# Another order for the softmax differences, the counting steps and a product on POOL

## The chip, the cores and the metric

The kernel runs on one core of a Trainium2 chip. The metric is the device time of one execution in microseconds (us); all times below are in us unless marked ns. TensorE is called PE (its weight loads PEld), VectorE DVE, ScalarE ACT, GpSimd POOL and SyncE SP. L12 is line 12 of the kernel.

## The reference, cut to what matters

Two mixers read the same x (2048 tokens, 512 columns, 32 heads of 16) and a gate per token blends them.

```
g = sigmoid((x * gate_w).sum(-1))
# A: linear attention, phi = softmax(p) beside softmax(-p), over 16 columns a head
phi_q, phi_k = ...
kv = einsum("bhsf,bhsd->bhfd", phi_k, v);  z = einsum("bhsf->bhf", phi_k)
den = einsum("bhqf,bhf->bhq", phi_q, z) + 1e-6
a = (einsum("bhqf,bhfd->bhqd", phi_q, kv) / den) @ wo
# B: 32 heads choose one expert of 16 x 16 each, by the best score of either half
act = gelu(einsum("nd,nhkd->nhk", x, u[best]));  b = sum of act * v[best] over heads
out = g * a + (1 - g) * b
```

## The kernel before, in words

The tokens are 16 tiles of 128. A first part (to about 130) folds the weights and gathers kv and z over all tiles. The second part, which the change touches, is a loop over tiles in which the stages of different tiles overlap. The order on every engine is the order of the program text, written out by hand; each engine works through its own queue and waits at semaphores.

For one tile t the work is:

- PE multiplies x by the folded query weights (`front_q`, tile `pq`, 12 matmuls of 512 columns), by the expert scores (`front_s`, two halves `s`, 12 each) and by the expert inputs and the gate (`front_p`, `pp`, 12 of 258 columns).
- `soft_in` (L670) makes the dual softmax's inputs with `softmax_diffs` (L111) on DVE: maximum (L115), minimum (L117), high difference p - max (L119), low difference min - p (L121). Between these four steps it calls a function `step`, by which other work is dealt in. `soft_exp` (L685) is two exponentials on ACT, one for each difference. `soft_w` (L691) is two products with z on POOL (`w`), one for each half. `soft_sum` (L695) sums the exponentials, `soft_y` (L705) sums w, both on DVE. `soft_p` (L700) makes 1e-6 times the product of both sums, as a third column beside two. `soft_b` (L707) turns these into the weight of each half: a product (L713), a sum over three columns (L715), a reciprocal (L717) and a product with the gate (L719) on DVE, then two products over the exponentials on POOL (L726).
- `planes`, `join`, `mid_num`: ACT splits the weighted exponentials into 16-bit planes (L758), SP transposes them by DMA, ACT joins them (L768), PE multiplies by kv (L777, `oT`). `num_hi` (L784, ACT) and `num_lo` (L790, DVE) split the result into a high and a low part for the output product.
- `best` (L734, L735) on DVE finds where each head's score is its maximum, once for each half. `turn_eq` (L741) transposes this by DMA into `et`, and `mid_mask` (L798, `mk`) on PE turns it into bit masks. `count` (L802 to L835) is a chain of 17 small DVE steps that counts, for each of the 256 experts, how many heads chose it. `step(t, n)` runs n steps of this chain and `drain(t)` the rest.
- `gelu_pre` (ACT), `gelu_in` (POOL, L653), `gelu_act` (ACT, L657 to L659) and `gelu_out` (POOL, L663) make the gelu of all 256 experts. `coef` (L839) on POOL multiplies it by the count. `c_planes` (L844), `c_join` (L851, L855) and `back_cl` (L876, DVE) turn, join and split this coefficient.
- `back` is 18 matmuls of the output (L888, L895, tile `po`), `store` (L912) copies it out.

A stage `turned(a)` (L971) does the softmax of tile a, the scores of tile n = a + 1, the counting, gelu and coefficient of tile b = a - 1 and the output of earlier tiles (z = a - 2). Of the 18 matmuls of an output some are put off: each stage up to 7 does 15 of them, each from 8 on 18. Five counting steps of tile a run within `soft_b(a)`; the twelve others run in the next stage within `soft_in`, dealt out by `dealt` (L960): after the maximum the gate reciprocal (L649), five steps and `back_cl` (L876), after the minimum five, after the high difference two.

On POOL the order of a stage is L653 of tile a, L691 twice, L663 and L839 of tile b, then L726 twice. `z_final` (L920) sums z over partitions on PE and copies it into `zb`, which `soft_w` reads.

Stages 0 and 1 and the tail (tile 15 with what is left of 13 and 14) are written out beside the loop and call `soft_in` without dealt work (in stage 15 counting steps follow it).

Of the kernel before, what the change touches and what calls it, by code (L numbers as in the profile page):

```python
# [15 lines left out]
AF = mybir.ActivationFunctionType  # L16
ALU = mybir.AluOpType
AX = mybir.AxisListType
# [17 lines left out]
def mix_kernel(ctx, tc, xT, wqT, wkT, wv, wphi, wo, wq, kk, ug, ev, cst, out):  # L36
    nc = tc.nc
    pe, dve, act, pool, sp = nc.tensor, nc.vector, nc.scalar, nc.gpsimd, nc.sync
# [4 lines left out]
    def mm_bank(name):  # L43
        return psum.tile([P, 512], F32, tag="mm", bufs=4, name=name)

    def tr_bank(name):
        return psum.tile([P, 512], F32, tag="tr", bufs=3, name=name)
# [27 lines left out]
    def x_of(t):  # L75
        first = max(f for f in SEC if f <= t)
        return tuple(xt[i, first][:, t - first] for i in range(2))
# [30 lines left out]
    def proj(o, t, wh, wl, c0, c1, ks=range(NK)):  # L108
        mm3(o, [(*xs(t, k), wh[:, k, c0:c1], wl[:, k, c0:c1]) for k in ks], ks[0] == 0, ks[-1] == NK - 1)
# [58 lines left out]
    class Sums:  # L168
        h = ((gh, gl), x_of(NT - 1))
# [152 lines left out]
    st8 = {t: {} for t in range(NT)}  # L322

    def front_s(t, half):
        e = st8[t]
        e[half] = mm_bank(f"s{half}_{t}")
        proj(e[half], t, sh, sl, 512 * half, 512 * half + 512)
# [141 lines left out]
    for t in range(5, NT - 1, 2):  # L469
# [14 lines left out]
        a = pks[t] = mm_bank(f"pk{t}")  # L484
        prod(a, tile_of(t, 0), b11, True)
        b = mm_bank(f"pu{t}")
# [23 lines left out]
        c = mm_bank(f"pv{t}")  # L510
# [65 lines left out]
    t = NT - 1  # L576
# [33 lines left out]
    zb = w2.tile([P, 1024], F32, name="zb", bufs=1)  # L610
    chains = {}

    def step(t, n=1):
        for _ in range(n):
            if t in chains and next(chains[t], None) is None:
                del chains[t]

    def drain(t):
        while t in chains:
            step(t)  # L620
# [22 lines left out]
    def gelu_pre(t):  # L643
        gelu_gate(t)
        gelu_rest(t)

    def gate(t):
        gs = st8[t]["g"]
        yield dve.reciprocal(gs[:, 2:3], gs[:, 1:2])  # L649
# [11 lines left out]
    def gelu_out(t):  # L661
        px, x2 = st8[t]["G"], st8[t]["x2"]
        pool.tensor_tensor(px, x2, px, op=ALU.mult)  # L663
# [16 lines left out]
    pair = lambda a: a.rearrange("p (h s) -> p h s", s=2)  # L680
# [6 lines left out]
    def soft_w(t):  # L687
        e = st8[t]
        e["w"] = w2.tile([P, 1024], F32, tag="w", bufs=1, name=f"w{t}")
        for i in range(2):  # L690
            pool.tensor_tensor(hs(e["w"], i), hs(e["ph"], i), hs(zb, i), op=ALU.mult)  # L691
# [2 lines left out]
        e = st8[t]  # L694
        dve.tensor_reduce(pair(e["st"][:, 64:128])[:, :, 1 - i], hs(e["ph"], i), axis=AX.X, op=ALU.add)  # L695

    def soft_p(t):
        st = st8[t]["st"]
        sm = pair(st[:, 64:128])
        dve.scalar_tensor_tensor(st[:, 128:224].rearrange("p (h c) -> p h c", c=3)[:, :, 2], sm[:, :, 0], 1e-6,  # L700
                                 sm[:, :, 1], op0=ALU.mult, op1=ALU.mult)

    def soft_y(t, i):
        e = st8[t]
        dve.tensor_reduce(pair(e["st"][:, 224:288])[:, :, i], hs(e["w"], i), axis=AX.X, op=ALU.add)  # L705

    def soft_b(t, step=step):  # L707
        e = st8[t]
        d, st = e["ph"], e["st"]
        sm, y, n_ = pair(st[:, 64:128]), pair(st[:, 224:288]), st[:, 288:320]  # L710
        q3 = st[:, 128:224].rearrange("p (h c) -> p h c", c=3)
        step(t)
        dve.tensor_tensor(q3[:, :, 0:2], y, sm, op=ALU.mult)  # L713
        step(t)
        dve.tensor_reduce(n_, q3, axis=AX.X, op=ALU.add)  # L715
        step(t)
        dve.reciprocal(n_, n_)  # L717
        step(t)
        dve.scalar_tensor_tensor(y, sm, e["g"][:, 2:3], n_.unsqueeze(2).to_broadcast([P, H, 2]),  # L719
                                 op0=ALU.mult, op1=ALU.mult)  # L720
        r = st[:, 224:288]
        step(t)
        for i, s_ in enumerate(halves):
            eng = dve if t == NT - 1 else pool
            gs_ = slice(32 * i, 32 * i + 32)
            eng.tensor_tensor(g64(d)[:, gs_], g64(d)[:, gs_], r[:, gs_].unsqueeze(2).to_broadcast([P, 32, F]), op=ALU.mult)  # L726
# [110 lines left out]
    def coef(t):  # L837
        e = st8[t]
        (pool if t < NT - 1 else dve).tensor_tensor(e["C"], e["C"], e["G"], op=ALU.mult)  # L839
# [34 lines left out]
    def back_cl(t, eng=dve):  # L874
        ch, cl, o = st8[t]["c"]
        eng.tensor_tensor(cl, o[:, :2 * P], ch, op=ALU.subtract)  # L876
# [43 lines left out]
    def z_final(zh, zl):  # L920
        for i, s_ in enumerate(halves):
            o = tr_bank("z")
            pe.matmul(o, neg, zh[i], start=True, stop=False)
            pe.matmul(o, neg, zl[i], start=False, stop=True)
            act.copy(zb[:, s_], o)

    def wo_load():
        both = late.tile([P, 2, D], F32, tag="d", name="rawo2")
# [29 lines left out]
    z_final(zh, zl)  # L958
    gelu_rest(0)
    def dealt(a, b, z):  # L960
        def first():
            for _ in gate(a):
                step(b)
            step(b, 4)
            if z >= 0:
                back_cl(z, dve)

        moves = iter((first, lambda: step(b, 5), lambda: step(b, 2), lambda: None))
        return lambda: next(moves)()

    def turned(a):  # L971
        n, b, z = a + 1, a - 1, a - 2
        owed = min(18, 3 * max(0, a - DEFER))
        left = min(18, 3 * max(0, a - DEFER + 1))
        if a == 2:
            mid_num(z)
            num_hi(z)
            gelu_pre(a)
        planes(b, 0)
        c_join(z)  # L980
        planes(b, 1)
        front_q(a)
        if owed:
            back(z - 1, owed)
            store(z - 1)
        gelu_in(a)
        if a == 2:
            num_lo(z)
        soft_in(a, dealt(a, b, z))
        drain(b)  # L990
        gelu_act(a)
        front_s(n, 0)
        if a < 5:
            if a == 2:
                front_s(n, 1)
            else:
                mid_num(z)
                num_hi(z)
            if a == 3:
                front_s(n, 1)  # L1000
            mid_mask(a)
            if a > 3:
                front_s(n, 1)
            soft_exp(a)
        else:
            soft_exp(a)
            mid_num(z)
            num_hi(z)
            mid_mask(a)
            front_s(n, 1)  # L1010
        soft_w(a)
        soft_sum(a, 0)
        soft_sum(a, 1)
        if a > 2:
            num_lo(z)
        front_p(n, False)
        if left < 18:
            back(z, 18 - left)
        best(n, 0)
        soft_y(a, 0)  # L1020
        soft_y(a, 1)
        soft_p(a)
        join(b)
        gelu_out(b)
        coef(b)
        c_planes(b)
        soft_b(a)
        best(n, 1)
        turn_eq(n)
        gelu_pre(n)  # L1030

    for a in range(NT - 1):
        n, b, z = a + 1, a - 1, a - 2
        if a > 1:
            turned(a)
            continue
        B, Z = b >= 0, z >= 0
        if a == 1:
            front_q(a)
            v15 = vproj(NT - 1)  # L1040
            act.copy(woh[3], rawo[3])
            planes(b, 0)
            v15()
            planes(b, 1)
        gelu_in(a)
        for _ in gate(a):
            pass
        if B:
            soft_in(a)
            dve.tensor_tensor(wol[3], rawo[3], woh[3], op=ALU.subtract)  # L1050
            step(b, 3)
            soft_exp(a)
            front_s(n, 0)
            mid_mask(a)
            kvacc(NT - 1)
            kv_final()
            cl_.close()
            w4 = ctx.enter_context(tc_pool("w4", "right"))
        else:
            gelu_act(a)  # L1060
        if not B:
            pass
        front_s(n, 1)
        front_p(n, False)
        soft_w(a)
        if B:
            best(n, 0)
        soft_sum(a, 0)
        soft_sum(a, 1)
        if B:  # L1070
            drain(b)
            soft_y(a, 0)
            soft_y(a, 1)
            soft_p(a)
            join(b)
            gelu_out(b)
            coef(b)
            c_planes(b)
            gelu_act(a)
            soft_b(a)  # L1080
            best(n, 1)
            turn_eq(n)
        else:
            pool.tensor_tensor(wol[2], rawo[2], woh[2], op=ALU.subtract)
            step(a, 5)
            best(n, 0)
            best(n, 1)
            turn_eq(n)
            soft_y(a, 0)
            soft_y(a, 1)  # L1090
            soft_p(a)
            soft_b(a, lambda t: None)
            gelu_pre(n)
    a, b, z = NT - 1, NT - 2, NT - 3
# [11 lines left out]
    def both(*ts):  # L1106
        for t in ts:
            step(t)
# [32 lines left out]
    soft_y(a, 0)  # L1141
    step(b, 2)
    soft_y(a, 1)
    soft_p(a)
    soft_b(a, lambda t: both(b, a))
    drain(b)
    coef(b)
# [85 lines left out]
```

## Time and profile before

| | us |
|---|---|
| median of 3 runs | 374.69 |
| lowest and highest | 374.16, 375.67 |
| the profiled execution | 375.6 |
| its span, first to last instruction | 373.8 |
| mean granted PE clock | 0.995 |
| busy: PE, DVE, ACT, POOL | 363.2, 338.2, 257.7, 205.2 |

A row of an order of time reads: start, duration, engine, line, operation, tile written, tile read, shapes, count; in brackets the engine's idle time before it and what released it. Where two instructions of a kind follow each other they stand in one row with x2 and their common duration. A matmul's end is modelled, so the pace of PE is read from the starts. A row on DVE can begin a little before the one ahead of it ends, so what an instruction costs its engine is also read from starts. Records of POOL are rough.

### The profile page before, as it was taken

Reading aid. Unit: us, or ns where it says so; the run is one execution under the profiler, and the core shown is the slowest. Engines: PE = TensorE matmul, PEld = TensorE weight load, DVE = VectorE, ACT = ScalarE, POOL = GpSimd, SP = SyncE. Lnnn points to the kernel's source line nnn. Section 1 sums busy time; section 2 is a strip of 40 time slices with the busy share of each in tenths; the row PEclk is TensorE's granted clock in tenths of the full one; section 3 lists DMA queues with packets and bytes.
Section 4 is the critical chain, followed back from the end, with each engine's and each line's share of the span. In section 5 each row is a group of like instructions: output and inputs, shape, how many; then the busy total and the mean of one; then the engine's idle time right before and its main releaser. Section 6 shows DMA issues by size and latency. Waiting matters only on the chain.

```text
span 373.8 us, 8800 instructions
## 1 busy us (share of the span) xinstructions
PE 363.2 (97%) x3426; PEld 284.0 (76%) x3426; DVE 338.2 (90%) x757; ACT 257.7 (69%) x457; POOL 205.2 (55%) x207
## 2 busy tenths in 40 slices
PE   8999999999989999999999999999999999999696
PEld 4766767777858878887787788878878888888476
DVE  4679999999788889999999999999999999999983
ACT  4585678876654776778687668767767776787843
POOL 1079989988846846444544445437426435454800
PEclk9999999999999999999999999999999999999899
DMA  7867888657882214044263442361551532522612
GB/s 269 317 243 264 278 257 228 198 145 283 289 164 86 70 20 82 20 84 83 60 114 70 72 112 50 80 128 26 102 116 27 114 82 61 113 63 68 98 44 84
DMA packets 74729, 47.32 MB, mean 127 GB/s; under 512 B 66240, under 2 KB 67136, under 8 KB 72384
## 3 DMA queue, kind: packets, MB, share of 16 engines
q1 hardware_dynamic: 73824, 45.89, 46.9%
q10 hardware_dynamic: 864, 0.87, 0.8%
q8 instruction: 27, 0.44, 0.5%
q14 instruction: 14, 0.11, 0.1%
HBM read 26.43 MB, written 4.19 MB: 82 GB/s over the span
## 4 chain that ended last, share of the span: by engine, by line
PE 68%; DVE 18%; DMA 4%; issue 4%; POOL 3%; ACT 2%; ACTq 0%; POOLq 0%
PE po L888 9%; PE pk L459 5%; PE po L895 4%; PE s L56 4%; PE s L57 4%; PE s L58 4%; PE ws L292 4%; PE pu L459 4%; PE pq L57 2%; PE pq L56 2%; PE pq L58 2%; DMA et<-eq 2%; PE pe L459 2%; PE kvacc L283 2%; PE pv L459 2%
## 5 line engine op out<-in xcount | busy, mean ns | idle before, releaser
L691 POOL TENSOR_TENSOR w<-d,zb 128x512 f32<-128x512 f32 x32 | 41.1, 1304 | 71.2 <-ACT d L685 71.2
L56 PE MATMUL s<-sh,xh 128*128 128x512 f32 x128 | 51.3, 400 | 0.0
L57 PE MATMUL s<-sl,xh 128*128 128x512 f32 x128 | 50.0, 390 | 0.0
L726 POOL TENSOR_TENSOR d<-d,st 128x512 f32<-128x512 f32 x30 | 31.2, 1063 | 34.0 <-DVE st L719 32.6
L58 PE MATMUL s<-sh,xl 128*128 128x512 f32 x128 | 49.8, 389 | 0.0
L758 ACT COPY pl<-d 128x1024 uint16<-128x1024 uint16 x30 | 31.3, 1044 | 20.7 <-POOL d L726 20.7
L685 ACT ACTIVATE d<-d 128x512 f32<-128x512 f32 x32 | 20.0, 631 | 28.5 <-DVE d L119 20.3
L768 ACT COPY pt<-tp 128x1024 uint16<-128x1024 uint16 x30 | 39.0, 1374 | 0.0
L276 POOL TENSOR_TENSOR d<-d,st 128x1024 f32<-128x1024 f32 x16 | 32.0, 2001 | 10.5 <-DVE st L272 7.4
L58 PEld LDWEIGHTS s<-sh,xl 128*128 128x128 f32 x128 | 24.0, 188 | 5.1
L56 PEld LDWEIGHTS s<-sh,xh 128*128 128x128 f32 x128 | 24.0, 188 | 4.8 <-ACT ctj L851 0.2
L57 PEld LDWEIGHTS s<-sl,xh 128*128 128x128 f32 x128 | 24.1, 188 | 4.5
L56 PE MATMUL pq<-wah,xh 128*128 128x512 f32 x64 | 25.2, 393 | 0.0
L156 DVE TENSOR_TENSOR xl<-xr,xh 128x512 fp32r<-128x512 f32 (+2 forms) x17 | 23.5, 1397 | 1.7 <-ACT xh L152 1.6
L58 PE MATMUL pq<-wah,xl 128*128 128x512 f32 x64 | 25.0, 390 | 0.0
L57 PE MATMUL pq<-wal,xh 128*128 128x512 f32 x64 | 25.0, 390 | 0.0
L735 DVE TENSOR_TENSOR eq<-s,mx 128x512 bf16<-128x512 f32 x32 | 22.1, 691 | 1.1
L695 DVE TENSOR_REDUCE st<-d 128x32 f32<-128x512 f32 x32 | 21.6, 681 | 1.3
L734 DVE TENSOR_REDUCE mx<-s 128x32 f32<-128x512 f32 x32 | 21.8, 680 | 0.0
L271 DVE TENSOR_REDUCE st<-d 128x64 f32<-128x1024 f32 x16 | 19.3, 1209 | 2.2 <-ACT d L267 2.2
L267 ACT ACTIVATE d<-d 128x1024 f32<-128x1024 f32 x16 | 17.0, 1065 | 5.8 <-DVE d L121 5.8
L705 DVE TENSOR_REDUCE st<-w 128x32 f32<-128x512 f32 x32 | 20.5, 676 | 0.6 <-POOL w L691 0.6
(273 smaller groups left out, 1121.8 us busy)
## 6 DMA issues: line engine op xcount, KB each, us to landing
wq<-wq SPq DMA_DIRECT2D x16, 1024.0 KB, 6.0
xr<-xT SPq DMA_DIRECT2D x15, 256.0 KB, 5.2
y<-ot SPq DMA_DIRECT2D x15, 256.0 KB, 2.4
rawk<-wkT SPq DMA_DIRECT2D x1, 1024.0 KB, 6.5
rawq<-wqT SPq DMA_DIRECT2D x1, 1024.0 KB, 6.8
rawu<-ug SPq DMA_DIRECT2D x2, 258.0 KB, 6.1
rawv<-wv ACTq DMA_DIRECT2D x2, 256.0 KB, 4.6
rawv<-wv SPq DMA_DIRECT2D x2, 256.0 KB, 5.8
```

What stands on the lines that cost most here:

```text
L56: pe.matmul(o, ah, bh, start=(first and i == 0), stop=False)
L57: pe.matmul(o, ah, bl, start=False, stop=False)
L58: pe.matmul(o, al, bh, start=False, stop=(last and i == n - 1))
L156: dve.tensor_tensor(l[:, ks], rawx[t][:, ks], h[:, ks], op=ALU.subtract)
L276: pool.tensor_tensor(g64(d), g64(d), b64(st[:, 128:192]), op=ALU.mult)
L459: pe.matmul(o, x_, w_, start=(first and i + j == 0), stop=(i == 1 and j == 2), skip_group_check=True)
L691: pool.tensor_tensor(hs(e["w"], i), hs(e["ph"], i), hs(zb, i), op=ALU.mult)
L726: eng.tensor_tensor(g64(d)[:, gs_], g64(d)[:, gs_], r[:, gs_].unsqueeze(2).to_broadcast([P, 32, F]), op=ALU.mult)
L735: dve.tensor_tensor(e["eq"][:, 512 * half:512 * half + 512].rearrange("p (h f) -> p h f", f=F), p3, mx.unsqueeze(2).to_broadcast([P, H, F] ...
L758: act.copy(pl, e["ph"][:, halves[i]].bitcast(U16).rearrange("p (c j) -> p j c", j=2))
L768: act.copy(p16[:, :, 4 * i:4 * i + 4, :], e["tp"][i].rearrange("p (j g) n -> p j g n", j=2))
L888: pe.matmul(po, a, b, start=(i == 0), stop=False)
```

## The change

It reorders and it leaves one instruction out.

- In the loop, `dealt` hands out the work in another way: nothing after the maximum; the gate reciprocal alone after the minimum; two counting steps after the high difference; after the low difference one counting step, `back_cl` and all the other steps. The high difference thus directly follows maximum, minimum and reciprocal.
- `gelu_out(b)` and `coef(b)` move ahead of `soft_w(a)`. On POOL the order of a stage becomes L653, L663, L839, L691 twice, L726 twice (lines of before).
- The 1e-6 of the denominator is no longer made of the two sums (`soft_p` is gone in all tiles, the sum L715 runs over two columns). Half of it is added to each z by the copy in `z_final`, since the two softmaxes of a head sum to 2.

```
-    def soft_p(t):
-        dve.scalar_tensor_tensor(st[:, 128:224].rearrange("p (h c) -> p h c", c=3)[:, :, 2], sm[:, :, 0], 1e-6,
-                                 sm[:, :, 1], op0=ALU.mult, op1=ALU.mult)
...
-        q3 = st[:, 128:224].rearrange("p (h c) -> p h c", c=3)
+        q2 = pair(st[:, 128:192])
-        dve.tensor_tensor(q3[:, :, 0:2], y, sm, op=ALU.mult)
+        dve.tensor_tensor(q2, y, sm, op=ALU.mult)
-        dve.tensor_reduce(n_, q3, axis=AX.X, op=ALU.add)
+        dve.tensor_reduce(n_, q2, axis=AX.X, op=ALU.add)
...
-            act.copy(zb[:, s_], o)
+            act.activation(zb[:, s_], o, AF.Copy, bias=0.5e-6)
...
     def dealt(a, b, z):
-        def first():
-            for _ in gate(a):
-                step(b)
-            step(b, 4)
-            if z >= 0:
-                back_cl(z, dve)
-        moves = iter((first, lambda: step(b, 5), lambda: step(b, 2), lambda: None))
+        def after_min():
+            for _ in gate(a):
+                pass
+        def after_high():
+            step(b, 2)
+        def after_low():
+            step(b)
+            back_cl(z, dve)
+            drain(b)
+        moves = iter((lambda: None, after_min, after_high, after_low))
         return lambda: next(moves)()
...
         soft_in(a, dealt(a, b, z))
-        drain(b)
...
+        gelu_out(b)
+        coef(b)
         soft_w(a)
...
         soft_y(a, 1)
-        soft_p(a)
         join(b)
-        gelu_out(b)
-        coef(b)
         c_planes(b)
```

More of the change, by code (lines that the diff above doesn't have):

```diff
@@ L695, in soft_sum @@
         dve.tensor_reduce(pair(e["st"][:, 64:128])[:, :, 1 - i], hs(e["ph"], i), axis=AX.X, op=ALU.add)
-    def soft_p(t):
-        st = st8[t]["st"]
-        sm = pair(st[:, 64:128])
-        dve.scalar_tensor_tensor(st[:, 128:224].rearrange("p (h c) -> p h c", c=3)[:, :, 2], sm[:, :, 0], 1e-6,
-                                 sm[:, :, 1], op0=ALU.mult, op1=ALU.mult)
     def soft_y(t, i):
@@ L1073, in mix_kernel @@
             soft_y(a, 1)
-            soft_p(a)
             join(b)
@@ L1090, in mix_kernel @@
             soft_y(a, 1)
-            soft_p(a)
             soft_b(a, lambda t: None)
@@ L1143, in mix_kernel @@
     soft_y(a, 1)
-    soft_p(a)
     soft_b(a, lambda t: both(b, a))
```

## The prediction

> **What bounds the kernel now.** I read, in this order, the busy time of the engines, the table by windows, the order of time on DVE, POOL, PE and ACT, and the chain that ended last.
>
> ```profile
> PE 363.2 (97%) x3426; PEld 284.0 (76%) x3426; DVE 338.2 (90%) x757; ACT 257.7 (69%) x457; POOL 205.2 (55%) x207
> 187.48:202.07 14.59, 14.59 (x107) 12.02 (x106) 14.11 (x39) 10.72 (x21) 6.78 (x8) 1.00 0.44 82
> 347.60:360.00 12.40, 8.97 (x99) 6.72 (x99) 12.33 (x36) 9.21 (x16) 6.44 (x8) 0.86 0.51 86
> ```
>
> The last two lines are windows: length, then busy time of PE, PEld, DVE, ACT and POOL, then the granted clock. In a stage of the main loop PE and DVE are both full. Right after the loop, from 347.60 on, DVE is still full, while PE idles and its clock falls to 0.86. So it has to be asked who leads whom. DVE in stage 4, and the same line a stage later and at the start of the tail:
>
> ```profile
> 186.88 0.68 DVE L115 TENSOR_REDUCE st<-pq 128x32 f32<-128x512 f32 x1
> 187.78 0.89 DVE L820 TENSOR_TENSOR X<-m 128x256 uint32<-128x256 uint32 x1
> 193.54 0.68 DVE L121 TENSOR_TENSOR d<-st,pq 128x512 f32<-128x512 f32 x1
> 194.14 1.46 DVE L695 TENSOR_REDUCE st<-d 128x32 f32<-128x512 f32 x2
> 195.52 0.74 DVE L790 TENSOR_TENSOR xl<-oT,xh 128x256 fp32r<-128x256 f32 x2
> 197.50 1.27 DVE L705 TENSOR_REDUCE st<-w 128x32 f32<-128x512 f32 x2
> 198.69 0.19 DVE L700 SCALAR_TENSOR_TENSOR st<-st 128x32 f32<-128x32 f32 x1
> 198.79 0.21 DVE L807 CAST sa<-mk 128x64 uint16<-128x64 f32 x1
> 201.48 0.68 DVE L115 TENSOR_REDUCE st<-pq 128x32 f32<-128x512 f32 x1
> 347.57 0.67 DVE L115 TENSOR_REDUCE st<-pq 128x32 f32<-128x512 f32 x1
> ```
>
> A DVE stage lasts 201.48 - 186.88 = 14.60, and from stage 4 to the tail (347.57) there are eleven of 14.61: a metronome with no wait in it. PE over the same stretch:
>
> ```profile
> 179.88 0.39 PE L888 MATMUL po<-wbh,xh 128*128 128x512 f32 x1
> 180.11 0.40 PE L888 MATMUL po<-wbl,xh 128*128 128x512 f32 x1
> 181.39 0.73 PE L888 MATMUL po<-t1h,xl 128*128 128x512 f32 x2 [0.89 <-DVE xl L790]
> 182.43 0.39 PE L56 MATMUL pq<-wah,xh 128*128 128x512 f32 x1
> 196.48 0.39 PE L56 MATMUL pq<-wah,xh 128*128 128x512 f32 x1
> 208.90 0.29 PE L57 MATMUL pp<-ul,xh 128*128 128x258 f32 x1
> 209.02 0.29 PE L58 MATMUL pp<-uh,xl 128*128 128x258 f32 x1
> 209.79 0.50 PE L888 MATMUL po<-t1h,xh 128*128 128x512 f32 x1 [0.48 <-ACT xh L784]
> 269.00 0.39 PE L56 MATMUL pq<-wah,xh 128*128 128x512 f32 x1
> 342.63 0.39 PE L56 MATMUL pq<-wah,xh 128*128 128x512 f32 x1
> 345.14 0.39 PE L58 MATMUL pq<-wah,xl 128*128 128x512 f32 x1
> 351.82 0.38 PE L798 MATMUL mk<-wm,et 128*128 128x16 bf16 x8 [3.43 <-DMA et<-eq]
> 353.06 0.63 PE L895 MATMUL po<-eh,ch 128*128 128x512 f32 x1
> 353.49 0.63 PE L895 MATMUL po<-el,ch 128*128 128x512 f32 x1
> ```
>
> An early PE stage, which carries 15 products of the output, takes 196.48 - 182.43 = 14.05. A late one carries 18 and takes (342.63 - 269.00) / 5 = 14.73. So DVE leads up to stage 7 and PE, at its own full pace, after it. A product follows another after 0.23 (179.88 to 180.11), a short one after 0.12 (208.90 to 209.02). PE's idle time before the tail is two stalls: 181.39 - 180.11 - 0.23 = 1.05 (the low part from DVE came late) and 209.79 - 209.02 - 0.12 = 0.65 (the high part from ACT). The scores of tile 15 end at 345.14 + 0.39 = 345.53 on PE, but DVE takes them up at 347.57, 2.0 behind. The tail then waits for DVE twice over: PE stands 3.43 until the transposed maxima of tile 15 arrive, and afterwards it runs products 0.43 apart (353.06 to 353.49) instead of 0.23.
>
> **The change, part by part.** *High differences earlier (L119 behind L117, L121 two counting steps later).* No instruction is added; the same 12 counting steps, the gate reciprocal and the low coefficient part are dealt out in another order, and as many of them as before follow directly on their own source (nine, by the code), so the order by itself costs nothing. What changes is whom they meet:
>
> ```profile
> L820 DVE TENSOR_TENSOR X<-m x15: 424/895/997, 147.1 to 350.7; 128x256 uint32<-128x256 uint32 x15
> 187.65 0.74 POOL L653 TENSOR_TENSOR x<-x,px 128x256 f32<-128x256 f32 x1
> 193.71 2.56 POOL L691 TENSOR_TENSOR w<-d,zb 128x512 f32<-128x512 f32 x2 [5.32 <-ACT d L685]
> 196.22 0.75 POOL L663 TENSOR_TENSOR px<-x,px 128x256 f32<-128x256 f32 x1
> 197.05 0.74 POOL L839 TENSOR_TENSOR cf<-cf,px 128x256 f32<-128x256 f32 x1
> 359.39 0.42 DVE L835 TENSOR_TENSOR cf<-X 128x256 f32<-128x256 uint8 x1
> 359.95 0.74 POOL L839 TENSOR_TENSOR cf<-cf,px 128x256 f32<-128x256 f32 x1 [4.90 <-DVE cf L835]
> ```
>
> L820 takes 0.424 at its fastest and 0.895 at the median (the first row: fastest, median, slowest). At 187.78 it starts while POOL's gelu product L653 runs (187.65 to 188.39) and ends at 188.67, its short time after POOL is through. In the new order two reductions and one difference come ahead (0.60 each, as from 193.54 to 194.14), the gate reciprocal and L813 (0.3 together), so L820 starts some 2.1 after L115, at about 188.97 on this stage's scale. That gains 0.47.
>
> But the gelu output product L663 now follows L653 without a wait, at about 188.34 to 189.09, and the step L813 ahead of L820 comes at 188.75. If it is held as L820 was, whose end was 0.28 after POOL's, it loses 0.2. Bounds: 0 (POOL already through, as when DVE waits for PE) and 0.35. I take 0.2 where DVE leads, nothing where it waits for PE. The Trainium skill, "SBUF — State Buffer", Who interferes with whom, says that a Vector instruction with two SBUF inputs and a GpSimd instruction that reads SBUF exclude each other for the whole instruction. By that L813 would lose the 0.35 and the DVE stage below would be 14.17; the trace agrees on the blocking but shows L820's release 0.14 sooner than POOL's record ends.
>
> *Exponentials earlier.* The pair of sums L695 takes 1.38 to its successor (194.14 to 195.52), the pair L705 only 1.19 (197.50 to 198.69), because the second sum waits for the second exponential. In the new order ACT gets both differences over 3 us before the sums: 0.18 gained.
>
> *soft_p gone, L715 over 64 in place of 96 columns.* L700 starts 0.10 ahead of L807, so dropping it saves 0.10 and not its 0.19, since neighbours overlap; 32 columns fewer save about 0.03, an estimate from the 0.60 that 512 columns take. This holds in all 16 tiles. Adding 0.5e-6 to z happens once, inside a copy that ACT makes anyway: 0, and 0.1 at most.
>
> *Coefficient ahead of the softmax weights.* POOL's L663 and L839 move ahead of L691, and L839 waits for the last counting step L835. Queued behind it on POOL are both halves of L691, and DVE's L705 waits for those. From the end of L835: 0.14 to the start of L839 (359.39 + 0.42 to 359.95), 0.83 to the next instruction (as from 196.22 to 197.05), 2.56 for the pair: w complete at 3.53. DVE wants the second half after the sums (1.20), the low part and the next tile's maximum (195.52 to 197.50, 1.98) and the first y sum (0.60), less 0.08 overlap: 3.70. It fits by 0.2, so 0; in stage 2, where the low part is elsewhere, it misses by about 0.5, once. c_planes, on ACT behind join, and its transpose on SP come no later than before.
>
> A DVE stage thus becomes 14.60 - 0.47 + 0.20 - 0.18 - 0.13 = 14.02. That is below PE's 14.05 and 14.73: **PE becomes the bound** of the whole loop. Over stages 3 to 14 DVE would gain 12 x 0.58 = 7.0, far more than the 2.0 that it lags; the rest is not cashed.
>
> *Where it ends.* PE's two stalls go (low part and high part both come over 1 us sooner): -1.7, bounds 0 and -2.0. DVE takes the scores of tile 15 at 345.53 - 1.7 = 343.8 plus 0.05: 3.7 sooner than 347.57. If the stalls stay, it is 2.0. Then the tail, with these rows:
>
> ```profile
> DMA to landing us min/median/max: 2.7/2.7/4.4
> 364.41 0.75 DVE L790 TENSOR_TENSOR xl<-oT,xh 128x256 fp32r<-128x256 f32 x2 [0.84 <-ACT xh L784]
> 360.72 0.62 ACT L844 COPY plc<-cf 128x512 uint16<-128x512 uint16 x1 [1.22 <-POOL cf L839]
> 362.04 1.07 ACT L751 COPY pt<-pt 128x512 f32<-128x512 f32 x2 [0.70 <-PE pt L749]
> ```
>
> The maxima of tile 15 do not need its scores, so they leave DVE near 342.9 (343.85 - 14.73 for L115 of stage 14, and 13.82 for a stage of DVE's in which L813 is not held), and their transpose, by the first row 2.7 to 4.4 on its way, lands at 345.6 to 347.3. PE wants it at 351.82 - 3.43 - 1.7 = 346.7 and so stands 0.6 at most instead of 3.43. A stall of 0.89 (at 181.39) was followed by products at the full pace, so I also count the slow ones as cured: PE alone could be over 5 us sooner. DVE and ACT can't: L835 moves by 3.7 + 0.1 = 3.8, with it coefficient, L844 and L751 on ACT. There the 0.70 that ACT now waits for PE goes too, since PE is ahead, and the 0.84 of DVE behind it. So the last output tile comes 3.8 + 0.7 = **4.5 us** sooner. The profiled execution took 375.6 (span 373.8), 0.9 over the median 374.69 of runs from 374.16 to 375.67; its span would be 369.3 and it would take 371.1, and the median 370.2.
>
> **Rivals.** *PE keeps its stalls* (the low and high parts stay late, or a bank comes free late). For it: PE has no other slack to give. Against it: both releasers move by more than the stalls. Then DVE gains its 2.0 lag alone: 2.0 + 0.1 + 0.7 = 2.8, median 371.9. 0.18.
>
> *The stall only moves house.* The change doesn't do what it says: counting stays in POOL's way, all of L663 falls on L813, L820 or a neighbour, and the gain is the sums and soft_p alone with most of it eaten: 0.13 to 0.2 a stage, 1.6 to 2.4 over 12, plus 0.8: 372.3 to 371.5. Against it: L663 ends 0.12 into L820 at most. 0.08.
>
> *POOL's weights come too late.* L839 stands in front of L691, and the slack is 0.2. Each 0.1 that the pair lands later than 3.70 costs 0.1 in every stage; from 0.58 on the DVE stage is longer than 14.60. If the pair took 3.7 in place of 2.56, L705 would wait 1.0: stage 15.0, +0.4 x 12 = 4.8, less 0.1: 379.4, slower. For it: L691 varies already (1.3 a piece against L653's 0.74 for half the columns is fair, no more); against it: no two-input DVE operation stands beside it. 0.04. A milder wait of 0.4 to 0.5, which eats the gain and leaves about 374, has 0.06.
>
> **How the numbers follow.** Main case 0.64, with its own range 368.6 (stalls 2.0, tail free by another 0.8) to 371.2 (PE's clock stays low, transposes at 4.4). The range 368.6 to 372.8 takes in nearly all of it, the first two rivals, and leaves out the last two. About 0.5%, 1.9 us, can be told from no change. Faster by more: main, first rival, most of the second, 0.87. Same: 0.09. Slower: 0.04.
>
> **What would show it.** L820 at 0.42 in all stages and L813 at 0.2 to 0.4; L695's pair at 1.27; no L700; POOL's order L653, L663, L839, L691 and L691's wait released by POOL or DVE; L705 with no idle time before it. DVE should wait before L115 for PE's pq in late stages, and the PE stage stay at 14.73. The two stalls at 181 and 209 should be gone, and mk in the tail should wait under 1 us at a clock near 1. A DVE stage still at 14.4 or more, L705 waiting for w, or PE waiting for xl or xh in every stage would make it wrong.

## The result, and the profile after

The changed kernel takes 369.14 (median of 6 runs, 368.66 to 370.68); the kernel before, run beside it, 374.98 (374.16 to 375.67). The ratio is 0.9849, 95% interval 0.9826 to 0.9873: 1.5% faster, 5.8 us between the medians. Lines from `soft_y` on have moved up by six: L807 is the L813 of before, L814 the L820, L784 the L790, L792 the L798, L833 the L839.

The page's busy times, then two windows of the loop (an early stage and a late one; length, then busy PE, PEld, DVE, ACT, POOL, then the clock) and 3 us after the scores of tile 15:

```profile
PE 361.4 (98%) x3426; PEld 282.8 (77%) x3426; DVE 329.8 (90%) x741; ACT 256.3 (70%) x457; POOL 205.8 (56%) x207
180.07:194.13 14.06, 14.06 (x105) 11.56 (x103) 13.68 (x38) 10.34 (x21) 6.72 (x8) 1.00 0.44 85
295.16:309.89 14.73, 14.73 (x109) 12.12 (x108) 13.50 (x39) 10.66 (x20) 6.72 (x7) 1.00 0.36 82
342.23:345.23 3.00, 3.00 (x51) 2.14 (x50) 2.95 (x6) 2.11 (x4) 1.72 (x3) 1.00 0.80 165
```

A late stage is now PE's 14.73, with DVE busy for 13.50 of it. DVE's share on the page is 90% as before, since the span shrank with its work: the share alone would not have told that the bound has moved. The order of time on DVE in stage 4 and at the start of the tail:

```profile
184.39 0.68 DVE L115 TENSOR_REDUCE st<-pq 128x32 f32<-128x512 f32 x1
185.66 0.68 DVE L119 TENSOR_TENSOR d<-pq,st 128x512 f32<-128x512 f32 x1
186.25 0.48 DVE L807 TENSOR_TENSOR m<-sa 128x32 uint32<-128x32 uint32 x1
186.76 0.43 DVE L814 TENSOR_TENSOR X<-m 128x256 uint32<-128x256 uint32 x1
191.47 1.27 DVE L695 TENSOR_REDUCE st<-d 128x32 f32<-128x512 f32 x2
198.48 0.68 DVE L115 TENSOR_REDUCE st<-pq 128x32 f32<-128x512 f32 x1
342.27 0.69 DVE L115 TENSOR_REDUCE st<-pq 128x32 f32<-128x512 f32 x1 [0.78 <-PE pq L58]
358.07 0.75 DVE L784 TENSOR_TENSOR xl<-oT,xh 128x256 fp32r<-128x256 f32 x2
```

The stage is 198.48 - 184.39 = 14.09. The counting step that took 0.89 takes 0.43, the pair of sums 1.27 for 1.46, and the step ahead, L807, pays 0.48 for 0.19. At tile 15 DVE now waits for PE (0.78), where it was 2.0 late. On POOL and PE:

```profile
185.23 0.75 POOL L653 TENSOR_TENSOR x<-x,px 128x256 f32<-128x256 f32 x1
185.93 0.76 POOL L663 TENSOR_TENSOR px<-x,px 128x256 f32<-128x256 f32 x1
191.69 0.74 POOL L833 TENSOR_TENSOR cf<-cf,px 128x256 f32<-128x256 f32 x1 [5.01 <-DVE cf L829]
192.39 2.55 POOL L691 TENSOR_TENSOR w<-d,zb 128x512 f32<-128x512 f32 x2
179.04 0.73 PE L882 MATMUL po<-t1h,xl 128*128 128x512 f32 x2 [0.21 <-DVE xl L784]
344.43 0.67 PE L771 MATMUL oT<-pt,kvb 64*32 64x128 f32 x32
345.03 0.36 PE L792 MATMUL mk<-wm,et 128*128 128x16 bf16 x8
345.56 0.40 PE L882 MATMUL po<-wbh,xl 128*128 128x512 f32 x1
345.80 0.39 PE L889 MATMUL po<-eh,ch 128*128 128x512 f32 x1
```

L663 runs until 186.69, across L807's start; the coefficient product stands 5.01 for the last counting step, and the weights L691 follow it at once. The stall of PE at 181 has shrunk from 0.89 to 0.21, that at 209 is gone, and the mask matmuls of tile 15 (mk) no longer wait: the products behind them come 0.23 apart (345.56, 345.80).

To see where the time went I cut each profiled execution at two marks on PE, the first matmul of `pq` for tile 0 and for tile 15. All kernels of the study are in the table; the rest is the span less the two parts before it (spans are read to 0.1, so it is good to 0.05), and the last column has all timed runs.

| kernel | first part | loop | rest | span | median (shortest to longest) |
|---|---|---|---|---|---|
| before | 126.52 | 216.11 | 31.17 | 373.8 | 374.98 (374.16 to 375.67) |
| after | 124.82 | 214.52 | 27.96 | 367.3 | 369.14 (368.66 to 370.68) |
| e0, after again | 125.06 | 214.49 | 27.95 | 367.5 | 369.26 (368.85 to 370.19) |
| e1, 1e-6 on DVE again | 125.06 | 214.96 | 28.08 | 368.1 | 369.94 (369.43 to 371.50) |
| e2, before, 1e-6 in z | 124.25 | 215.44 | 28.81 | 368.5 | 370.62 (370.33 to 372.35) |
| e3, products back behind | 126.50 | 233.84 | 34.26 | 394.6 | 395.63 (394.22 to 396.37) |
| e4, old dealing | 124.58 | 218.69 | 31.93 | 375.2 | 377.49 (377.02 to 379.36) |
| e5, gelu in its own stage | 124.94 | 214.20 | 27.96 | 367.1 | 368.81 (368.76 to 368.86) |
| e6, load in stages 11 to 14 | 124.42 | 214.50 | 27.98 | 366.9 | 368.95 (368.65 to 370.20) |
| e7, load in stages 3 to 9 | 124.37 | 214.51 | 28.02 | 366.9 | 368.92 (368.70 to 369.46) |
| e8, after, DVE first | 124.84 | 214.54 | 28.02 | 367.4 | 369.26 (368.86 to 369.36) |
| e9, after, POOL first | 126.39 | 214.51 | 28.00 | 368.9 | 370.71 (370.65 to 371.04) |
| e10, before, DVE first | 125.09 | 215.92 | 32.79 | 373.8 | 374.72 (374.03 to 376.10) |
| e11, e5 and DVE first | 124.88 | 214.26 | 27.96 | 367.1 | 368.86 (368.82 to 368.91) |

Between the profiles of before and after, the loop became 1.59 shorter and the rest 3.2; the 1.70 of the first part, which the change doesn't touch, is another matter (e8 to e10).

### The profile page after: what moved, and what is told of

Its sections match the earlier page's. It is cut to its first block, busy times and chain, and to the rows that moved or that the text cites. A ratio compares the mean times of both kernels' runs of the same rounds, so it can differ in the third digit from the quotient of the medians.

```text
span 367.3 us, 8802 instructions
## 1 busy us (share of the span) xinstructions
PE 361.4 (98%) x3426; PEld 282.8 (77%) x3426; DVE 329.8 (90%) x741; ACT 256.3 (70%) x457; POOL 205.8 (56%) x207
## 4 chain that ended last, share of the span: by engine, by line
PE 78%; DVE 12%; POOL 3%; ACT 2%; issue 2%; DMA 2%; ACTq 0%; POOLq 0%
PE po L882 8%; PE s L56 6%; PE s L57 6%; PE s L58 6%; PE pk L459 5%; PE po L889 5%; PE pu L459 4%; PE ws L292 4%; PE pq L57 3%; PE pq L58 3%; PE pq L56 3%; PE oT L771 2%; PE pe L459 2%; PE kvacc L283 2%; PE pv L459 2%
## 5 line engine op out<-in xcount | busy, mean ns | idle before, releaser
L833 POOL TENSOR_TENSOR cf<-cf,px 128x256 f32<-128x256 f32 x15 | 11.1, 740 | 75.7 <-DVE cf L829 75.7
L691 POOL TENSOR_TENSOR w<-d,zb 128x512 f32<-128x512 f32 x32 | 41.0, 1304 | 2.7 <-ACT d L685 2.7
L276 POOL TENSOR_TENSOR d<-d,st 128x1024 f32<-128x1024 f32 x16 | 32.6, 2036 | 8.5 <-ACT d L267 6.5
L156 DVE TENSOR_TENSOR xl<-xr,xh 128x512 fp32r<-128x512 f32 (+2 forms) x17 | 21.7, 1290 | 1.7 <-ACT xh L152 1.6
L699 DVE TENSOR_REDUCE st<-w 128x32 f32<-128x512 f32 x32 | 20.6, 676 | 0.9 <-POOL w L691 0.9
L695 DVE TENSOR_REDUCE st<-d 128x32 f32<-128x512 f32 x32 | 20.4, 677 | 0.0
```

Of the source, the lines that this page charges most:

```text
L276: pool.tensor_tensor(g64(d), g64(d), b64(st[:, 128:192]), op=ALU.mult)
```

## Experiments

**e1: the changed kernel with the 1e-6 made on DVE again.** The sum over three columns is back too.

```
+        soft_p(a)                      # in all tiles
-            act.activation(zb[:, s_], o, AF.Copy, bias=0.5e-6)
+            act.copy(zb[:, s_], o)
```

> The kernel after the change, with the 1e-6 made on DVE from the two sums again (soft_p in every tile, three columns in the sum). My theory: PE bounds the late stages, so DVE work of 0.13 a stage is free there. The DVE stage is 14.08 + 0.13 = 14.21 up to the stage where it catches up with PE (some two stages later than in the changed kernel), the late stages stay at 14.73, and only the tail pays: 0.1 to 0.4 over the changed kernel's 369.1, so 369.2 to 369.5. Rival, every DVE instruction counts: 16 x 0.13 = 2.1 more, 371.2.

Measured 369.94, 0.7 to 0.8 over the changed kernel: above my figure and well under the rival's 2.1. The DVE stage is 14.22 up to stage 11 and 14.73 from stage 13, as expected. In the profiles the loop grew by 0.44 and the rest by 0.1. The loop's part is the early stall, which I had left out: PE at 179.73 waits 0.68 for the low part, where it waited 0.21. So the instruction costs time at one stall and in the tail, not in every stage. The reordering without the smaller sum is worth 5.35 (375.29 for before in that set, 369.94 here), the smaller sum without the reordering 4.7 (e2), both together 5.8: the parts don't add, since either one is enough to take most of PE's wait out of the tail (0.93 left in e2, none in e1).

**e2: the kernel before with only the 1e-6 moved into z.** The edit is that of the change's diff (L697 to L715 and `z_final`) without the rest.

> The kernel before with only the 1e-6 moved into z (soft_p gone, two columns). My theory: there DVE leads up to stage 7 and lags PE by 2.0 at tile 15, so nearly all of 16 x 0.13 is cashed in the tail, and a little of ACT's and DVE's waits for PE behind it: 1.9 to 2.8 below the 375.0 of before, so 372.2 to 373.1; L820 stays at 0.89 and the DVE stage is 14.47. Rival, the whole gain is PE's two stalls and soft_p is worth nothing: 374.5 to 375.

Measured 370.62, lower than either theory had it. The DVE stage is 14.47 and L820 (L814 in this kernel) keeps its 0.89, as expected; the median fell by 4.7, not by 1.9 to 2.8. PE in the tail of this kernel (mask matmuls, then products two rows on):

```profile
346.39 0.36 PE L792 MATMUL mk<-wm,et 128*128 128x16 bf16 x8 [0.93 <-DMA et<-eq]
347.15 0.39 PE L889 MATMUL po<-eh,ch 128*128 128x512 f32 x1
347.38 0.39 PE L889 MATMUL po<-el,ch 128*128 128x512 f32 x1
```

The wait is 0.93 in place of 3.43, and the products come 0.23 apart. So moving DVE ahead by less than 2 us saved the wait and, with it, the slow products after it, which my expectation for this kernel had not counted although the prediction had. Like for like the profiles give 0.67 in the loop and 2.3 in the rest, 3.0. I put what is left of the 4.7 down to the first part and to the length of the slow stretch, both of which scatter (below); no run separates them here.

**e3: the changed kernel with gelu output and coefficient behind join again.**

```
-        gelu_out(b)
-        coef(b)
         soft_w(a)
...
         join(b)
+        gelu_out(b)
+        coef(b)
         c_planes(b)
```

> The kernel after with the gelu output and coefficient products back behind join, that is behind the softmax weights on POOL as before. My theory: the coefficient product, waiting for the last counting step, is what keeps POOL's two weight products (2.55 together) off the counting. Without it they start as soon as the first exponential is there, some 5.2 after the maximum, and the counting steps from then on (1.8 of work, all with two inputs or of the form that L826 is) are blocked, twice by 1.3. The DVE stage goes from 14.08 to 15.7 or 16.1, over 14.60 too, so slower than both: 388, between 382 and 394, with counting steps of over 1 us in the order of time on DVE. Rival, the place of the coefficient product doesn't matter and the order on DVE alone brings the gain: 369, with L807 at 0.19 in place of 0.48.

Measured 395.63, 26 over the changed kernel and 20 over before. The rival falls. The time is above my range of 382 to 394. DVE's counting in stage 3 of this kernel, and POOL beside it:

```profile
175.85 0.18 DVE L807 TENSOR_TENSOR m<-sa 128x32 uint32<-128x32 uint32 x1
179.57 0.23 DVE L824 TENSOR_SCALAR X<-T 128x128 uint32<-128x128 uint32 x1
179.83 1.20 DVE L825 TENSOR_SCALAR T<-T 128x128 uint32<-128x128 uint32 x1
181.07 1.26 DVE L826 TENSOR_TENSOR X<-X,T 128x256 uint16<-128x256 uint16 x1
182.37 0.83 DVE L829 TENSOR_TENSOR cf<-X 128x256 f32<-128x256 uint8 x1
179.62 2.57 POOL L691 TENSOR_TENSOR w<-d,zb 128x512 f32<-128x512 f32 x2 [4.11 <-ACT d L685]
182.14 0.78 POOL L663 TENSOR_TENSOR px<-x,px 128x256 f32<-128x256 f32 x1
```

The last three steps, 0.23, 0.29 and 0.42 in the changed kernel, take 1.20, 1.26 and 0.83: one is held by each half of L691 and one by L663, 2.35 together. From stage 5 on ACT makes the exponentials earlier in its stage, so L691 starts earlier (5.07 after the maximum in stage 7, 5.62 in stage 3), and the steps that are held are earlier ones; in stage 7:

```profile
243.89 1.52 DVE L823 TENSOR_TENSOR T<-X 128x256 uint16<-128x256 uint16 x1
245.45 1.21 DVE L824 TENSOR_SCALAR X<-T 128x128 uint32<-128x128 uint32 x1
246.70 0.67 DVE L825 TENSOR_SCALAR T<-T 128x128 uint32<-128x128 uint32 x1
```

Against 0.42, 0.23 and 0.23 in the changed kernel that is 2.5 more. L807 gives back 0.3, since L663 no longer stands beside it, and the stage is 16.3, 2.2 over 14.08. What I had too low is this stage (15.7 or 16.1) and its number: stage 2 is hit too (15.53 for 13.53). From tile 0 to tile 15 DVE takes 25.3 longer than in the changed kernel. The edit moves two products at once; that the coefficient product is the one that matters is shown by e5, where the gelu product stands behind L691 and nothing collides.

**e4: the changed kernel with the old dealing of the counting steps.**

```
     def dealt(a, b, z):
+        def first():
+            for _ in gate(a):
+                step(b)
+            step(b, 4)
...
+        moves = iter((first, lambda: step(b, 5), lambda: step(b, 2), lambda: None))
...
         soft_in(a, dealt(a, b, z))
+        drain(b)
```

> The kernel after with the old dealing of the counting steps (after maximum, minimum and high difference), but with the two products ahead of the softmax weights. My theory: POOL's gelu input and output products now stand back to back beside the first counting steps, which are held by both: DVE stage 14.60 - 0.13 + 0.3 to 0.7 = 14.8 to 15.2, so slower than before: 379, between 376 and 383. Rival, the products are harmless and the order of the differences is worth only what it saves at L820: like the kernel with the 1e-6 alone, 372.2 to 373.1.

Measured 377.49, ratio to before 1.0064 (1.0042 to 1.0086): slower, as expected, and the stage is 14.96. Here L814 takes 0.90 and L817, which follows it, 0.71 for 0.29, while L653 and L663 run back to back. Set against e2, which has neither half of the reordering, the product move alone costs 6.9 (377.49 for 370.62) and the new dealing alone 25 (e3, 395.63), while both together gain 1.5 (369.14). Neither half is a change by itself.

**e0, e5, e6, e7: what is DVE's time worth in the changed kernel?** e0 is the changed kernel itself, for the three others.

> The changed kernel once more, as the measure for the three beside it on the same chip. Both theories: 369.1, between 368.5 and 370.

Measured 369.26.

```
+        if a == 2:
-        gelu_out(b)
+            gelu_out(b)
         coef(b)
         soft_w(a)
+        gelu_out(a)
...
-    gelu_out(b)                        # in the tail
```

> The kernel after, with the gelu output product of tile a right behind the softmax weights of its own stage, so that POOL is idle when the counting step L807 comes. My theory: L807 falls from 0.48 to 0.19 and the DVE stage from 14.08 to 13.8, but PE's 14.05 and 14.73 bound the stages, so next to nothing: 368.6 to 369.2, 0 to 0.5 under the changed kernel. Rival, DVE still leads where its stage is the longer one: 8 stages x 0.28 = 2.2, or 12 x 0.28 = 3.4 less: 366.9 to 365.7.

Measured 368.81, 0.45 under e0, whose shortest run (368.85) lies among those of e5; the profiles show the difference more clearly. L807 is at 0.18 and the early DVE stage at 13.79, 0.28 shorter; the loop became 0.29 shorter, once and not in every stage, and PE's stage 3 went from 14.62 to 14.38, since its last early stall is gone. The rival's 2.2 falls. The coefficient product is now the only one ahead of the softmax weights, and it alone keeps them off the counting.

e6 and e7 add the same line under two conditions:

```
         turn_eq(n)
+        if a > 10:                     # e7: if 2 < a < 10:
+            dve.tensor_reduce(st8[a]["st"][:, 192:224], hs(st8[a]["w"], 0), axis=AX.X, op=ALU.add)
```

> The kernel after with one more reduction on DVE (0.60, into unused columns) in each of the stages 11 to 14. My theory: DVE waits 0.65 for PE in each of these stages, so 4 x 0.60 = 2.4 of work is hidden: 0 to 0.3 over the changed kernel, and the DVE stage still 14.73. Rival, DVE leads all through: +2.4, 371.5.

Measured 368.95: 2.4 us of DVE work hidden, as expected.

> The kernel after with the same extra reduction in each of the stages 3 to 9, seven times. My theory: there DVE leads by a hair (14.08 against PE's 14.05), so the stages become 14.68, DVE's lag at stage 10 rises from 0.25 by 4.2 to about 4.45, melts by 0.65 in each late stage to about 1.2 at tile 15, and the time grows by 1.2 to 2.5: 370.3 to 371.6. If PE bounds everywhere: 369.1 to 369.4. If DVE leads everywhere: +4.2, 373.3.

Measured 368.92: my +1.2 to +2.5 didn't come; it fits "PE bounds everywhere". The trace tells why. DVE in stage 5 of e7 (L1028 is the added reduction):

```profile
198.33 0.68 DVE L1028 TENSOR_REDUCE st<-w 128x32 f32<-128x512 f32 x1
198.92 0.68 DVE L115 TENSOR_REDUCE st<-pq 128x32 f32<-128x512 f32 x1
200.19 0.68 DVE L119 TENSOR_TENSOR d<-pq,st 128x512 f32<-128x512 f32 x1
200.77 0.18 DVE L807 TENSOR_TENSOR m<-sa 128x32 uint32<-128x32 uint32 x1
```

The reduction moves L807 to after L663's end, so L807 is back at 0.18 and the stage grows to 14.38, not to 14.68. DVE's lag behind PE rises to 3.4 at stage 8, PE never waits for it, and by stage 14 it has melted to 0.03. Some 2.1 us (7 x 0.31) of real load on the early stages cost nothing. The dearer case that I had forecast, 0.60 a stage, was thus not tried.

**e8, e9, e10, e11: the scatter of the first part.** Of the ten profiles up to here eight have a first part of 124.2 to 125.1, and before and e3 one of 126.5. In the first part one low part on DVE (L156 of tile 15) and one softmax product on POOL (L276) come within 0.1 of each other. Before:

```profile
109.90 2.41 DVE L156 TENSOR_TENSOR xl<-xr,xh 128x512 fp32r<-128x512 f32 x1 [0.22 <-ACT xh L152]
109.83 1.94 POOL L276 TENSOR_TENSOR d<-d,st 128x1024 f32<-128x1024 f32 x1
```

After:

```profile
109.71 0.69 DVE L156 TENSOR_TENSOR xl<-xr,xh 128x512 fp32r<-128x512 f32 x1 [0.24 <-ACT xh L152]
109.72 2.49 POOL L276 TENSOR_TENSOR d<-d,st 128x1024 f32<-128x1024 f32 x1
```

In the one POOL starts 0.07 ahead and DVE takes 1.72 longer; in the other DVE starts 0.01 ahead and POOL takes 0.55 longer. Two edits settle who is first (e8 and e10 the upper, e9 the lower):

```
+        if t == NT - 3:
+            pool.memset(rawx[NT - 1][:, 0, 0:1], 0.0)
         k_mult(t)
...
-            x_split(NT - 1)
+            x_high(NT - 1)
+            dve.tensor_reduce(zc, rawx[NT - 1]..., axis=AX.X, op=ALU.add)
+            x_low(NT - 1)
```

> The kernel after with one small memset on POOL ahead of the softmax product of tile 13 in the first part; it overwrites a column that DVE's low part of tile 15 (L156) reads, so POOL's product can only start when L156 is through. My theory: in the runs so far the first part ends at 124.2 to 125.1 or at 126.5, because L156 and that product of POOL come within 0.1 of each other and whichever starts first holds the other (L156 took 0.69 in the one case, 2.41 in the other). With DVE always first every execution is of the short kind: all between 368.6 and 369.5, none at 370 or over. Rival, the scatter has another cause: still some at 370 to 371.

> The kernel after with a reduction on DVE (0.60, into a tile that isn't in use yet) ahead of the same L156, so that POOL's product starts first. My theory: L156 takes over 2 us in every execution, pq of tile 0 begins at 126.4 or later, and all times are 370.3 to 371.2. Rival, the scatter has another cause: 369.1 to 369.8, the 0.6 at most.

Measured: e8 369.26, all runs between 368.86 and 369.36; e9 370.71, all between 370.65 and 371.04, with L156 at 2.28. Both as expected: the order of these two instructions, decided by less than 0.1 us, is worth 1.5 us, and the changed kernel's single runs at 370.19 and 370.68 are near that length. The added reduction isn't what lengthens e9: before and e3 don't have it, and their first part is as long (126.5 for 126.39).

> The kernel before with the same memset. My theory: all executions of the short kind, 373.8 to 374.4 in place of 374.2 to 376.5, and against the changed kernel with the memset the change itself is worth the 1.6 that the loop and the 3.2 that the tail became shorter: 4.8, 1.3%. Rival, the whole 5.8 between the medians is the change's: 374.9.

Measured 374.72, ratio to before 0.9998 (0.9981 to 1.0015): missed. Seven of twelve runs lie at 374.0 to 374.7 and the others reach 376.1, still a width of 2.1 (3.0 for the 17 runs of before beside it), and the median lies nearer to the rival's 374.9 than to my 373.8 to 374.4. The profiled one, with L156 at 0.69, has a rest of 32.79. PE there:

```profile
350.38 0.38 PE L800 MATMUL mk<-wm,et 128*128 128x16 bf16 x8 [3.62 <-DVE X L822]
352.05 0.63 PE L897 MATMUL po<-el,ch 128*128 128x512 f32 x1
352.47 0.63 PE L897 MATMUL po<-eh,ch 128*128 128x512 f32 x1
356.63 0.39 PE L890 MATMUL po<-wbh,xh 128*128 128x512 f32 x1
356.86 0.40 PE L890 MATMUL po<-wbl,xh 128*128 128x512 f32 x1
```

After the wait of 3.62 the products stay 0.43 apart until 356.3, some 13 of them; in before's own profile it was some 8, until 355.3. The kernel before thus has two sources of scatter, and the second, the length of the slow stretch, is seen in these two profiles but was not isolated by a run. The granted clocks of the twelve runs fit it: the five at 0.990 or 0.991 took 374.73 to 376.10 (median 375.62), the seven at 0.994 or 0.995 took 374.03 to 374.99 (median 374.41), so longer runs had PE at its low clock for longer. With the first source settled on both sides the change is worth 374.72 - 369.26 = 5.5, where I had expected 4.8.

> The kernel after with that memset and with the gelu output product of tile a in its own stage behind the softmax weights. My theory: both effects add, 0 to 0.3 and the long executions: 368.3 to 368.9 and all within 0.5. Rival: POOL's later product of tile 13 is missed in the loop: 369.2 or more.

Measured 368.86, all between 368.82 and 368.91: 0.4 under e8 of the same set. The ratios to before are 0.9835 (0.9815 to 0.9856) and, for e8, 0.9844 (0.9822 to 0.9865), so their intervals overlap. It has no run over 369, where the changed kernel has some at 370.2 and 370.7. But e5 without the memset was as short and as steady (368.81, all five runs between 368.76 and 368.86), so these runs don't show that the two effects add.

## Why the prediction was right

*DVE's stage.* Forecast 14.02, measured 14.08: L820 gained 0.46 (0.47), the sums 0.19 (0.18), L700 and the shorter sum 0.13 (0.13), and L813 lost 0.29 where I had taken 0.2 between bounds of 0 and 0.35. This is the one place where the rule of the Trainium skill ("SBUF — State Buffer", Who interferes with whom) and my reading of L820's row parted. L663 runs from 185.93 to 186.69 by its record, and L807 (0.19 by itself) ends at 186.73: it was let go 0.15 before POOL's record ended, as L820 had been. The trace agrees with the rule that they exclude each other. My 0.2 was too small because L807 came 0.44 before the end of that record, where I had put it at 0.34.

*PE becomes the bound.* Shown: DVE waits for pq from stage 11 on, a late stage stays at 14.73, and e6 and e7 hide 2.4 and 2.1 us of extra DVE work. Of the 7.0 that DVE could gain, only the 2.0 of lag and what PE's stalls released were cashed.

*PE's stalls.* Forecast 1.7 less in the loop, measured 1.59, but not from the same terms. The two stalls that I had counted gave 1.44: stage 3 went from 15.32 to 14.64, where a wait of 0.21 stayed, and stage 5 from 14.81 to 14.05. A third, of 0.18 in stage 9 (at 264.49, PE waiting for `et`), I had overlooked; it went too. So PE had three stalls before the tail, and that the sum came so near is in part luck. The second stall could go without DVE getting ahead of PE. ACT's high part of the result in stage 5, in before, after and e7:

```profile
209.39 0.62 ACT L784 CAST xh<-oT 128x256 fp32r<-128x256 f32 x2
203.97 0.62 ACT L778 CAST xh<-oT 128x256 fp32r<-128x256 f32 x2
203.81 0.62 ACT L778 CAST xh<-oT 128x256 fp32r<-128x256 f32 x2
```

It starts 7.91 after that stage's maximum in before (201.48) and 5.49 and 4.89 after it in the others (198.48, 198.92). In e7 DVE is further behind PE here than in before (5.25 from the start of `pq` to the maximum, for 5.00), and PE still doesn't wait. The earlier place of the exponentials, and with them of ACT's high part, within the stage is enough to take this stall away.

*The coefficient ahead of the weights.* Forecast: free, with 0.2 to spare. L691 is complete 3.4 after the last counting step, and L699 starts without idle time in the loop but for 0.32 in stage 2, where I had said 0.5. What I missed is what this move is for. I wrote that the new order of counting by itself costs nothing; e3 against e2 shows that it would cost 25 us, because exponentials that come earlier also start POOL's weights earlier, and ten counting steps now come after the low difference, so the weights run into the counting. The product that waits for L829 is the gate that holds them off. I had the two rows for it, L691 waiting for ACT and L820 held by POOL, and didn't put them together, since the change as a whole never shows the collision. That the change moved both together is, as far as my reasoning goes, luck.

*The tail.* The sum gave 2.8 there (4.5 less the 1.7 of the loop), the profiles 3.2. Mask matmuls and clock came out as said, no wait and a clock of 1. The chain that ended last runs, in after, from DVE's last counting step of tile 14 over POOL's coefficient to ACT, and from 356.48 on PE works to the end with no wait. The rows of after, and the last one of before (its others stand in the prediction):

```profile
354.00 0.41 DVE L829 TENSOR_TENSOR cf<-X 128x256 f32<-128x256 uint8 x1
355.32 0.62 ACT L838 COPY plc<-cf 128x512 uint16<-128x512 uint16 x1 [3.50 <-POOL cf L833]
355.84 1.07 ACT L745 COPY pt<-pt 128x512 f32<-128x512 f32 x2
357.50 0.65 ACT L778 CAST xh<-oT 128x256 fp32r<-128x256 f32 x2 [0.59 <-PE oT L771]
364.00 0.65 ACT L784 CAST xh<-oT 128x256 fp32r<-128x256 f32 x2 [0.89 <-PE oT L777]
```

With the 1.70 of the first part taken off, the maximum of tile 15 comes 3.6 sooner (forecast 3.7), the last counting step 3.7 (forecast 3.8) and ACT's copy L745, which no longer waits for PE, 4.5, as forecast. The 0.3 that I had missed lies behind it: the high part of the last tile comes 4.8 sooner, since ACT waits only 0.59 for PE there instead of 0.89.

*The total.* 370.2 was forecast and 369.14 came, in the range. Loop and rest in the profiles sum to 4.8, near the 4.5 of the forecast; the medians lie 5.8 apart. The prediction took the profile of before as typical in all its parts, and priced neither a first part that changes by 1.5 nor a slow stretch of 8 to 13 products; I have not separated how much of the last 1.0 belongs to which; e10 against e8, with the first part settled on both sides, still leaves 0.7 over the 4.8.

*Rivals.* PE kept 0.2 of its stalls; the stall at L820 did partly move house, to L807, at 0.29 of 0.46. POOL's weights were late once, by 0.32 in stage 2.

## What to carry to other kernels

Where two engines are both full, take each engine's period from the starts of the same line in successive stages, and the lag between them: the lag says how much of a saving on one is cashed, and at which later wait. An instruction that waits at the head of an in-order queue is not only a cost: here it keeps two others away from work they would hold up, so when moving one thing earlier, ask what else that lets start, and against whom it then runs. A short wait of PE can cost more than itself: look at the pace of the products after it.

## What was not expected of the hardware

Two instructions on DVE and POOL that both read SBUF start 0.01 to 0.07 us apart in the profiles of before and after, and whichever came second paid: DVE's took 1.72 longer than its 0.69, or POOL's 0.55 longer than its 1.94. With the order set by an edit (e8 and e9) the executions were 1.5 us apart. Between two POOL products that follow each other without a gap, DVE's waiting instruction got its turn each time (L825, L826 and L829 in stage 3 of e3, one behind each product). And after waits of 3.4 and 3.6 us PE ran at half pace for about 8 and about 13 products of 512 columns, after waits of 0.9 not at all.
